# Which score pairs of an attention kernel go to VectorE: 66 instead of 62

## The chip, the cores and the metric

The kernel runs on one core of one Trainium2 chip. The metric is the device time of one execution in microseconds (us); smaller is better. The core has five engines with a queue of instructions each: PE (TensorE, matmuls into PSUM), ScalarE (ACT), VectorE (DVE), GpSimd (POOL) and SyncE (SP, which here issues most of the DMAs). Each queue is processed in order; semaphores tie the queues together.

## The reference, cut to what matters

Two branches read the same input x (2048 tokens, width 640) and are mixed by a gate:

```
g = sigmoid(sum(x * gate_w))
a = q * (long_conv(k_shift * v, ssm_k) + k_shift * v * D)      # A: state-space branch, q = x
p = softmax(scores * 20**-0.5)                                 # B: attention, 32 heads of 20,
b = (p @ v) @ wo                                               #    one shared k and v head
out = g * a + (1 - g) * b
```

In branch B every one of the 32 heads has 2048 x 2048 scores, and each of them needs one exponential: 134 million in all. The change is about which engine computes some of them.

## The kernel before, in words

**Tiles, groups, pairs.** A *group* G (0 to 31) is four heads by 512 query tokens: eight groups of heads for each of four blocks of queries. Inside a group, j (0 to 15) runs over blocks of 128 key tokens and r (0 to 3) over the heads. A score tile (G, j, r) is 128 keys by 512 queries, so there are 32 x 16 x 4 = 2048 tiles. Two tiles of one (G, j) are a *pair*; there are 1024.

**The main path.** Scores are multiplied by PE (L1023) into PSUM, two banks at a time for one unit and three for the next. ScalarE takes the exponential of a whole unit in one instruction (L1055): three tiles (1536 columns) into the buffer ETA, two tiles (1024 columns) into ETB, in turn. PE then multiplies by v (L1097) and sums over j in one PSUM bank, bank 6; a column of ones in v gives the denominator. With the last j of a group the sum is copied to `acc` (L1151), the denominators go through a short chain of DMAs (den, scr_d, rbc), their reciprocals are taken (L1156), and L1163 multiplies them in.

**VectorE's share.** For the pairs that the table `DVE_J` names, two of the four tiles of (G, j) never go to ScalarE. PE writes their scores into a side bank, and VectorE computes the exponential with six instructions: L1085 twice (out of PSUM into dJ), L1088, L1090, L1092 (the exponent's bits and a polynomial), L1093 (the product, into ETd, of which there is one buffer). PE adds ETd to the sum whenever it is there (L1097), at the latest before the last j of the group. `DVE_J[G]` lists the j of group G. All other tiles are strung together over the group borders and cut into units:

```
if j in DVE_J[G]:
    mine, rest = order[:2], order[2:]
    self.on_dve[G, j] = tuple(sorted(rest))
    order = rest + mine
...
n = 2 if len(self.units) % 2 else 3
self.units.append(tiles[i:i + n])
```

**The side work.** Branch A runs beside attention: a shift convolution on PE (L1270), the transforms of five chunks of channels (L1336) whose results VectorE evacuates (X and K, L1347 to L1355), complex products on GpSimd (L1367), inverse transforms on PE (L1400) with evacuation on VectorE (L1410). Projections of the next queries (L949), the output projection of the finished query blocks (L1434, evacuated by L1437 into outsb, then stored), and of six of the last block's groups (L1187, evacuated by L1191) are side work too. After the last accumulation a closing sequence runs alone: L1201 to L1206 on VectorE normalise the last group, PE multiplies (L1211), VectorE combines (L1233), and the last four stores go out.

**The order.** The order of each queue is not written by hand. A planner in the kernel builds a graph of all operations, gives each a cost from a small formula and a priority, and plays them through; the order in which it placed them is the order of each queue. In time that PE has left it puts filler matmuls (L1482). So another table `DVE_J` changes the place of nearly all the side work on PE, VectorE, GpSimd and SyncE, though not what is computed. The main sequence of scores and exponentials stays as the table and the units give it.

## Time and profile before

| what | value |
|---|---|
| time, median of 5 runs | 918.82 us (912.05 to 920.36) |
| the profiled execution's own time | 912.05 us |
| its span, first to last instruction | 910.2 us |
| granted TensorE clock, mean | 0.998 |
| first exponential of the scores starts | 25.3 us |
| exponentials on ScalarE (L1055) | 385 into ETA, 385 into ETB |
| pairs on VectorE (L1093) | 62 |

A row of the profile names the source line, the engine, the operation, what it writes and reads, and how often it ran; behind the bars stand its busy time, the mean duration of one, and the idle time of the engine just before it with what ended that. The chain of waits is followed back from the last instruction. The five runs contain the profiled one, which was the shortest; the other four lie between 918.31 and 920.36 us.

### The profile page before, as it was taken

The page shows a single profiled execution, that of the slowest core. Times are in us where ns is not written, and L with a number is a line of the kernel's source. Part 1 is how long each engine was busy: PE and PEld are TensorE (multiplying, and loading weights), DVE is VectorE, ACT ScalarE, POOL GpSimd, SP SyncE. Part 2 cuts the span into 40 slices and gives each one's busy share as a digit, 9 for nine tenths or more (in the row PEclk, how much of TensorE's full clock was granted, in tenths as well). Part 3 has the DMA queues.
Part 4 walks back from the last instruction along what each step waited for, and adds up shares of the span by engine and source line. Part 5 has one row for each costly group of instructions (what it writes and reads, how often), then busy time and mean ns, then how long its engine had stood idle before and what let it go on. Part 6 is the DMA issues. An engine that isn't in the chain of part 4 may idle for free.

```text
span 910.2 us, 16382 instructions
## 1 busy us (share of the span) xinstructions
PE 864.5 (95%) x7015; PEld 352.6 (39%) x7015; DVE 609.6 (67%) x854; ACT 887.8 (98%) x794; POOL 369.8 (41%) x330
## 2 busy tenths in 40 slices
PE   7999999999999999999999999999999989998997
PEld 3344434444343343443343334444444434422232
DVE  5467564459978766866576766566488655886673
ACT  5999999999999999999999999999999999999995
POOL 2940055790434477033576404569505871000000
PEclk9999999999999999999999999999999999999999
DMA  7930300010000001000001010000000003011100
GB/s 162 205 128 9 64 21 19 14 30 18 20 19 14 19 16 35 19 19 19 13 15 35 28 46 19 13 12 15 19 19 19 13 6 103 13 35 63 42 27 30
DMA packets 58507, 32.69 MB, mean 36 GB/s; under 512 B 41154, under 2 KB 54466, under 8 KB 58434
## 3 DMA queue, kind: packets, MB, share of 16 engines
q1 hardware_dynamic: 56168, 31.05, 12.4%
q8 instruction: 55, 0.90, 0.4%
q10 hardware_dynamic: 2266, 0.59, 0.3%
q14 instruction: 18, 0.15, 0.1%
HBM read 18.01 MB, written 6.02 MB: 26 GB/s over the span
## 4 chain that ended last, share of the span: by engine, by line
ACT 70%; PE 27%; DVE 1%; DMA 1%; SPq 1%; issue 0%; DVEq 0%
ACT ETA L1055 42%; ACT ETB L1055 28%; PE ps L1023 8%; PE ps L1336 6%; PE ps L1097 5%; PE ps L1400 3%; PE ps L949 2%; PE ps L1270 1%; DVE ETd L1093 1%; DMA xT<-in_A_q_dram 1%; SPq L722 1%; PE ps L893 0%; PE ps L965 0%; PE ps L1482 0%; PE ps L1211 0%; DVE outsb L1233 0%
## 5 line engine op out<-in xcount | busy, mean ns | idle before, releaser
L1055 ACT ACTIVATE ETA<-ps 128x1536 bf16<-128x1536 f32 x385 | 570.4, 1482 | 2.1 <-PE ps L1023 1.0
L1055 ACT ACTIVATE ETB<-ps 128x1024 bf16<-128x1024 f32 x385 | 408.7, 1062 | 0.1
L1023 PE MATMUL ps<-qT,kT 21*128 21x512 bf16 x2048 | 303.5, 384 | 30.8 <-ACT ETA L1055 20.8
L1367 POOL TENSOR_TENSOR Pp<-X,K 128x512 f32<-128x512 bf16 x120 | 162.9, 1383 | 350.6 <-DVE K L1355 349.6
L1097 PE MATMUL ps<-ETA,vaug 128*32 128x512 bf16 x1155 | 195.6, 389 | 0.3 <-ACT ETB L1055 0.3
L1097 PE MATMUL ps<-ETB,vaug 128*32 128x512 bf16 x769 | 186.8, 389 | 0.0
L1023 PEld LDWEIGHTS ps<-qT,kT 21*128 21x128 bf16 x2048 | 75.2, 91 | 226.1 <-ACT ETA L1055 120.9
L1085 DVE TENSOR_SCALAR dJ<-ps 128x512 uint32<-128x512 f32 x124 | 85.2, 687 | 38.7 <-PE ps L1023 38.1
L1093 DVE SCALAR_TENSOR_TENSOR ETd<-dJ,dE 128x1024 bf16<-128x1024 f32 x62 | 85.8, 1384 | 24.1 <-PE ps L1097 23.8
L1090 DVE SCALAR_TENSOR_TENSOR dE<-dJ,dE 128x1024 f32<-128x1024 uint16 x62 | 82.9, 1337 | 0.3
L1092 DVE SCALAR_TENSOR_TENSOR dJ<-dJ 128x1024 f32<-128x1024 uint16 x62 | 81.5, 1314 | 0.2
L1367 POOL TENSOR_TENSOR AB<-Pp 128x256 bf16<-128x256 f32 x80 | 79.1, 989 | 5.3
L1400 PE MATMUL ps<-AB,Tcos 128*128 128x256 bf16 x320 | 78.1, 275 | 0.0
L1097 PEld LDWEIGHTS ps<-ETA,vaug 128*32 128x32 bf16 x1155 | 47.8, 93 | 66.2 <-issue 63.9
L1400 PE MATMUL ps<-AB,Tsin 128*128 128x256 bf16 x280 | 69.2, 275 | 0.0
L1097 PEld LDWEIGHTS ps<-ETB,vaug 128*32 128x32 bf16 x769 | 45.0, 93 | 43.8 <-issue 42.2
L1367 POOL TENSOR_TENSOR Pp<-Pp 128x512 f32<-128x512 f32 x40 | 58.1, 1453 | 2.9
L1088 DVE TENSOR_SCALAR dE<-dJ 128x1024 uint32<-128x1024 uint32 x62 | 53.6, 865 | 0.6
L1151 DVE COPY acc<-ps 128x512 f32<-128x512 f32 x31 | 21.4, 689 | 48.2 <-PE ps L1097 48.1
L1336 PE MATMUL ps<-ssm_kT,Tsin 128*128 128x256 bf16 x320 | 53.0, 275 | 0.0
L1336 PE MATMUL ps<-ssm_kT,Tcos 128*128 128x256 bf16 x320 | 51.8, 275 | 0.0
L1336 PE MATMUL ps<-kv,Tcos 128*128 128x256 bf16 x320 | 51.7, 275 | 0.0
(135 smaller groups left out, 849.7 us busy)
## 6 DMA issues: line engine op xcount, KB each, us to landing
rbc<-scr_d SPq DMA_DIRECT2D x31, 256.0 KB
scr_o<-oTn SPq DMA_DIRECT2D x24, 128.0 KB, 1.7
xn<-in_A_q_dram SPq DMA_DIRECT2D x4, 640.0 KB
kv<-in_A_v_dram SPq DMA_DIRECT2D x4, 640.0 KB, 4.6
out_dram<-outsb SPq DMA_DIRECT2D x14, 160.0 KB, 2.3
oTp<-scr_o SPq DMA_DIRECT2D x12, 160.0 KB, 2.3
wog<-in_B_wo_dram SPq DMA_DIRECT2D x4, 200.0 KB
wo<-in_B_wo_dram SPq DMA_DIRECT2D x4, 200.0 KB
```

The lines of the kernel that those rows point to most:

```text
L1023: return e.matmul(self.bank(bk), T["kT4"][32 * r:32 * r + 21, 128 * j:128 * j + 128], T[f"qT{G // 8 % 2}"][32 * r:32 * r + 21, G % 8, :], ...
L1055: op("act", lambda e: e.activation(et(n)[:, 0:w], self.ps[:, lo:lo + w], ACT.Exp, scale=SCALE), [("ps", base[n % 2] + k) for k in range(le ...
L1085: self.evac(gr, "dve", lambda e, bk, h=h: e.tensor_scalar(J[:, 512 * h:512 * h + 512], self.bank(bk), SCALE * LOG2E * 65536.0, EOFF * 6553 ...
L1088: V(lambda e: e.tensor_scalar(E[:, :], J[:, :], 7, 0x7F800000, ALU.logical_shift_left, ALU.bitwise_and), [kJ], ["dE"], c_fast(1024), **k)
L1090: V(lambda e: e.scalar_tensor_tensor(Ef, lo, ED, Ef, ALU.add, ALU.mult), [kJ, "dE"], ["dE"], c_ps(1024), **k)
L1092: V(lambda e: e.scalar_tensor_tensor(Jf, lo, EP, lo, ALU.add, ALU.mult), [kJ], [kJ], c_ps(1024), **k)
L1093: V(lambda e: e.scalar_tensor_tensor(T["ETd"][:, :], Jf, EQ, Ef, ALU.add, ALU.mult), [kJ, "dE"], ["ETd"], c_ps(1024), **k)
L1097: return op("pe", lambda e: e.matmul(self.bank(6)[32 * r:32 * r + 32, :], T["vaug"][:, j, :], src, start=(j == 0), stop=(j == NSC - 1), ti ...
L1151: self.dve(lambda e: e.tensor_copy(T["acc"][:, :], self.bank(6)), [("ps", 6)], ["acc"], c_ps(512), prio=-9000.0, name="acc")
L1336: o = self.mm(gr, lambda e, bk, lhs=lhs, rhs=rhs, comp=comp, n=n: e.matmul(self.bank(bk, 256, 256 * comp), lhs, rhs, start=(n == 0), stop= ...
L1367: f = lambda e: e.tensor_tensor(out, a, b, alu)
L1400: self.mm(gr, lambda e, bk, lhs=lhs, fc=fc, comp=comp, h=h: e.matmul(self.bank(bk, 256, 256 * h), lhs, AB[:, fc, :, comp, :], start=(fc == ...
```

## The change

Only the table `DVE_J` differs. It names 66 pairs instead of 62, and most groups name other j than before. The first five groups now name none (before, groups 3 and 5 named one each); groups 11, 18 and 29 name four (before, group 6 alone did); the other groups name one to three. The table was found by a search on the planner.

```
-DVE_J = [(), (), (), (6,), (), (2,), (3, 7, 11, 13), (2, 6, 11), (2, 9), (2, 9), (2, 9), (2, 9), (3, 8, 13), (2, 9), (2, 9), (2, 9), (2, 9), (2, 9), (4, 11), (2, 9), (3, 9), (2, 9), (2,), (3, 8, 13), (2, 9), (2, 7), (2, 9), (2, 7, 12), (3, 8, 13), (3, 9), (3, 8, 13), (2, 7, 12)]
+DVE_J = [(), (), (), (), (), (6,), (2, 9), (2, 9), (2, 9), (2, 9), (2, 9), (3, 7, 11, 13), (2, 9), (6,), (3, 8, 13), (2, 9), (3, 9), (2, 9), (3, 7, 11, 13), (2, 7, 12), (2, 7), (3, 9), (2, 7), (1, 5, 9), (2, 7, 12), (3, 8, 13), (4, 11), (2, 6, 11), (2, 6, 11), (1, 4, 8, 12), (2, 9), (1, 5, 9)]
```

The changed program's order has 66 x 2 = 132 score tiles off ScalarE instead of 124. Nothing else of the source moves; everything that the planner decides is placed anew.

## The prediction

> **What bounds the kernel now.** I read the page first (busy shares, the chain that ended last), then the ScalarE timeline in one quiet stretch and at the start, then the waits, then VectorE by stage, and last the end of the program.

> ```profile
> PE 864.5 (95%) x7015; PEld 352.6 (39%) x7015; DVE 609.6 (67%) x854; ACT 887.8 (98%) x794; POOL 369.8 (41%) x330
> ...
> ACT 70%; PE 27%; DVE 1%; DMA 1%; SPq 1%; issue 0%; DVEq 0%
> ...
> L1055 ACT ACTIVATE ETA<-ps 128x1536 bf16<-128x1536 f32 x385 | 570.4, 1482 | 2.1 <-PE ps L1023 1.0
> L1055 ACT ACTIVATE ETB<-ps 128x1024 bf16<-128x1024 f32 x385 | 408.7, 1062 | 0.1
> ```

> ScalarE is busy 98% of the span, and its two exponentials stood idle 2.1 and 0.1 us in all before 770 instructions. Nothing that VectorE or PE does in between is felt as long as this stays so. The chain's 27% on PE does not contradict it: matmuls of one unit lie between two exponentials while the previous exponential still runs.

> ```profile
> 810.35 1.47 ACT L1055 ACTIVATE ETA<-ps 128x1536 bf16<-128x1536 f32 x1
> 811.67 1.05 ACT L1055 ACTIVATE ETB<-ps 128x1024 bf16<-128x1024 f32 x1
> 812.61 1.46 ACT L1055 ACTIVATE ETA<-ps 128x1536 bf16<-128x1536 f32 x1
> ```

> Here the instructions overlap: a three-tile unit is followed after about 1.33 us (not 1.47), a two-tile unit after 0.9 to 0.94 us (not 1.05). So what an exponential costs is its distance to the next, not its duration. The view of the tile ETA has first and last start at 25.3 and 898.9 us: 384 steps of three plus two tiles in 873.6 us, 2.275 us for five tiles, 0.455 us for one.

> ```profile
> PEld ps L1023 <- ACT ETA L1055: 120.9, 355, 1.2
> ...
> PEld ps L1023 <- ACT ETB L1055: 84.3, 290, 0.8
> ...
> DVE acc L1151 <- PE ps L1097: 48.1, 21, 6.9
> ...
> DVE ETd L1093 <- PE ps L1097: 23.8, 25, 1.8
> ...
> ACT ETA L1055 <- PE ps L1023: 1.0, 2, 0.8
> ```

> PE waits for ScalarE, 205 us at the weight loads of the scores; ScalarE waits for PE twice. Nearly all of the 24 us that VectorE sat before ETd was for PE to consume the previous ETd: VectorE runs ahead of need.

> **The change part by part.**

> *ScalarE.* 62 pairs are 124 tiles off ScalarE, 66 are 132. The 2048-124 = 1924 tiles on ScalarE are now 385 units of three, 384 of two, and one last unit of one tile in ETB. The changed 2048-132 = 1916 = 383 x 5 + 1 are 383 units of three, 383 of two, and one last unit of one tile, now in ETA. The order of the changed program agrees: ScalarE's list differs only in its last instructions. Removed: two three-tile units and one two-tile unit: 2 x 1.33 + 0.94 = 3.6 us (8 x 0.455 = 3.64 gives the same). The last one-tile unit costs the same in either tile. All of this is on the path: **-3.6 us**.

> *VectorE.* Four more pairs, each two L1085, one L1088, L1090, L1092 and L1093. Groups of VectorE's instructions in two stretches, 795 to 880 us, where GpSimd is idle, and 480 to 580 us, where it works:

> ```profile
> L1085 DVE TENSOR_SCALAR dJ<-ps 128x512 uint32<-128x512 f32 x16 | 11.0, 690 | 3.7 <-PE ps L1023 3.7
> L1093 DVE SCALAR_TENSOR_TENSOR ETd<-dJ,dE 128x1024 bf16<-128x1024 f32 x9 | 11.0, 1221 | 3.7 <-PE ps L1097 3.7
> ```
> ```profile
> L1093 DVE SCALAR_TENSOR_TENSOR ETd<-dJ,dE 128x1024 bf16<-128x1024 f32 x7 | 9.8, 1405 | 2.2 <-PE ps L1097 2.1
> ...
> L1088 DVE TENSOR_SCALAR dE<-dJ 128x1024 uint32<-128x1024 uint32 x7 | 5.5, 787 | 0.0
> ```

> Quiet, a pair is 2 x 0.690 + 0.676 + 2 x 1.216 + 1.221 = 5.7 us; beside GpSimd 2 x 0.687 + 0.787 + 1.418 + 1.263 + 1.405 = 6.2 us. Four pairs: 23 to 25 us on an engine that is idle 910.2-609.6 = 300 us. What hides it is local: in a group with n pairs ScalarE needs (64-2n) x 0.455 us, 25.5 for four, 26.4 for three, 27.3 for two. I counted VectorE's instructions in the changed order from one copy of acc (L1151) to the next and priced them so. The fullest groups are 29 (four pairs, six output evacuations, GpSimd done by then): 23.9 us of 25.5; 19: 23.3 to 25.5 of 26.4; 18 (four pairs): 22.2 to 24.3 of 25.5; 25: 21.9 to 23.7 of 26.4. These durations overlap by nearly 0.1 us each, 2 us a group. The kernel before already has such a group: group 6, four pairs, 25.0 us by the same prices in 25.5, and from 199.8 to 226.4 us ScalarE was busy 26.55 of 26.60. So I take **0** for VectorE. Cover gone, a group that overruns delays ETd, then PE's last accumulation and the next scores, by the overrun: 0 to 1 us in each of four groups. It cannot gain: ScalarE does not wait for VectorE now.

> *PE.* No matmul is added. Each pair splits a four-row accumulation into two of two (+4 slots) and issues its two scores alone (+8), and three units of scores go (-3): nine slots. PE's filler matmuls (L1482) follow each other at 0.22 us (three busy 0.82, one 0.385), so 2.0 us, against 149 fillers left in the changed order (151 now), 33 us that PE idles deliberately. **0**; at most 2.0 us if not one of them hit free time.

> *GpSimd.* [...] Row first: beside GpSimd L1093 is 1405 against 1221 ns and L1088 787 against 676, so 0.5 us a pair, slowing but no exclusion. [...] The page's waits give the cover: GpSimd waited 349.6 us for the spectra (POOL Pp, DVE K). [...] I use the row.

> *SyncE.* In the changed order the first loads of oTp and wo stand between the den transfer of group 26 and its scr_d, and two rounds of them before rbc; now all stand behind rbc. Rounds started 2.5 to 4.2 us apart (755.1, 757.8, 762.0, 764.5), so that group's rbc is up to 6 us later; queued behind it is L1163 and all after it on VectorE. Normally acc is free long before the next copy, 26 us later. VectorE may stop 0 to 3 us there. I take 0 on ScalarE, 1 us as the upper end.

> *The end.* Now side work is over at 891 us and the closing sequence starts alone:

> ```profile
> 890.35 0.55 DVE L1191 SCALAR_TENSOR_TENSOR part<-ps,omgf,kv 128x320 f32<-128x320 f32 x1 [1.17 <-PE ps L1187]
> 901.39 0.72 DVE L1201 STREAM_TRANSPOSE acc<-ps 128x512 f32<-128x512 f32 x1 [10.49 <-PE ps L1097]
> ...
> 904.47 3.26 DVE L1233 SCALAR_TENSOR_TENSOR outsb<-ps,omgf,part 128x640 bf16<-128x640 f32 x4 [0.60 <-PE ps L1211]
> ```

> In the changed order eight half blocks of the output projection (L1434, 40 matmuls) have moved into the last group. Five L1434 stand between the last two accumulations on PE, where three fillers (0.82 us) stand now, and their evacuation L1437 directly before L1201. Nearest row: L1437, 547 ns. The matmuls (5 x 0.135 us, by columns from the filler's 0.22) fit the fillers' place; then the evacuation overlaps the wait for the last accumulation (0.5 us from exponential's end to L1201). Bounds 0 and 0.6 us, no gain possible, since L1201 waits for that accumulation anyway; I take **+0.2**, as most is covered. The fourth L1233 must wait for the store of the same outsb: a store lands 2.3 us after issue, L1233's fourth starts 5.5 us after L1201: 0, up to 1 us if stores queue.

> *Sum.* -3.6 + 0.2 = -3.4 us. The profiled execution took 912.05 us (span 910.2 and 1.9 around it): 908.6. Its four unprofiled companions took 918.3 to 920.4, and the median is 918.82; I carry the 6.8 us between as constant: **915.4 us**, -0.37%.

> **The rivals.** (1) *More than the sum.* Against the steps 1.33 and 0.904 (start to start, most of the steps) ScalarE loses some 16 us over the span in small hitches. If the new spread also smooths these by 2 us, the gain is 5 to 6 us: 913. Against: the groups lose 0.2 to 0.9 us each with no relation to their pairs. (2) *Gain eaten.* The upper ends above (VectorE 2, PE 1, SyncE 1) take it back: 917 to 919. (3) *Slower: the side work becomes the end.* The last inverse transform stands later in the order (128 L1400: now 45 in group 26 and 83 in 27; changed, 81 in 27 and 47 in 28), so the output projection runs to the last accumulation instead of ending 10.5 us before L1201. All its halves go through one PSUM bank: five matmuls of 0.135 us, their latency, an evacuation of 0.55: about 1.5 us a half. [...] For: no filler is left behind them, and GpSimd feeds them. Against: GpSimd finished at 755.07 with the first dependent inverse at 760.3, PE's last group carries 76 side matmuls of 0.135 us, 10 us, less than group 2 carries now (12 us by the same price), and of PE's eleven waits for outsb now the longest was 0.9 us. (4) *The change does less than it says*: excluded by the order.

> **How the numbers follow.** What a measurement here can tell from no change is about 0.5%, 4.6 us. Main case 0.67 (912.5 to 917.5), more 0.10, eaten 0.11, slower 0.12. Faster by over 0.5% (below 914.2): the better rival and a fifth of the main case, 0.23. Slower (above 923.4): 0.11. Within: 0.66. Range 910.8 to 920: the main case, the eaten one and part of rival 1, about 0.83; outside are rival 3 and a gain beyond 8 us.

> **What would show it.** Right: 383 + 383 full units, idle before ETA and ETB still under 4 us, five tiles still at 2.275, first exponential still at 25.3, last exponential 3.6 us earlier, L1201 within 0.7 us of it. Wrong: ScalarE waits for PE in groups 18, 19, 25 or 29, with PE waiting for ETd (VectorE overrun); L1163 waiting for rbc near 775 us (SyncE); L1201 more than 1 us behind the last exponential, with L1437 before it (rival 3).

## The result, and the profile after

The changed kernel takes 908.33 us (median of 27 executions, 907.17 to 913.05); the kernel before, on the same chip and in the same rounds, 917.78 us (48 executions, 909.96 to 929.49). The ratio is 0.992, 95% interval 0.9901 to 0.9939: the change is faster, by more than the forecast of 915.4 us said, and outside its range of 910.8 to 920 on the fast side. The medians stand 1.0% apart and the ratio says 0.8%, because the executions of before fall into two clusters (15 of the 48 at 912.5 us or less, 33 at 916.1 or more) and their median lies in the longer one; the means are 916.3 and 909.1. The ratio leaves out executions over 1.5% above the fastest of their kernel, here the one of 929.49 us.

The profiled execution of the changed kernel took 908.11 us (span 906.0), its mean granted TensorE clock was 0.999. From its page, the busy shares, the chain that ended last, and ScalarE's two groups of exponentials:

```profile
PE 863.2 (95%) x7013; PEld 350.7 (39%) x7013; DVE 632.4 (70%) x878; ACT 883.8 (98%) x791; POOL 380.1 (42%) x330
...
ACT 64%; PE 31%; DMA 2%; DVE 1%; SPq 1%; issue 0%; DVEq 0%
...
L1055 ACT ACTIVATE ETA<-ps 128x1536 bf16<-128x1536 f32 x384 | 571.0, 1487 | 3.4 <-PE ps L1097 2.1
L1055 ACT ACTIVATE ETB<-ps 128x1024 bf16<-128x1024 f32 x383 | 410.0, 1071 | 0.2 <-PE ps L1023 0.2
```

384 and 383 exponentials: 383 units of three, 383 of two, and the last single tile, as forecast. VectorE has gained 22.8 us of work (632.4 against 609.6); ScalarE still sits idle for only 3.6 us before 767 exponentials. By this page the kernel is what the forecast said it would be: bound by ScalarE, a little shorter.

The pair of profiles explains 3.9 us: 912.05 against 908.11. From the first exponential's start to the last one's end the two traces measure 875.58 us before and 873.19 after, so -2.4. The first exponential starts at 23.5 us instead of 25.3, which is not the change: the start of before had one stretch of 3.4 us at half the TensorE clock (12.6 to 16.0 us), and two further profiles of the changed kernel have it too, with a first exponential at 25.6 and 25.3. The rest, +0.2, lies behind the last exponential and outside the span. But the medians fell by 9.45 us. More than half of the gain lies in executions that the two profiles don't show. That is what the experiments had to find.

### The profile page after: what moved, and what is told of

It is laid out like the page before. It is cut to its first block, busy times and chain, and to the rows that moved or that the text cites. A ratio compares the mean times of both kernels' runs of the same rounds, so it can differ in the third digit from the quotient of the medians.

```text
span 906.0 us, 16396 instructions
## 1 busy us (share of the span) xinstructions
PE 863.2 (95%) x7013; PEld 350.7 (39%) x7013; DVE 632.4 (70%) x878; ACT 883.8 (98%) x791; POOL 380.1 (42%) x330
## 4 chain that ended last, share of the span: by engine, by line
ACT 64%; PE 31%; DMA 2%; DVE 1%; SPq 1%; issue 0%; DVEq 0%
ACT ETA L1055 39%; ACT ETB L1055 25%; PE ps L1023 9%; PE ps L1336 7%; PE ps L1097 6%; PE ps L1400 3%; PE ps L949 2%; PE ps L1270 1%; DMA rbc<-scr_d 1%; DMA xT<-in_A_q_dram 1%; PE ps L1434 1%; SPq L722 1%; PE ps L1187 1%; PE ps L893 0%; PE ps L965 0%
## 5 line engine op out<-in xcount | busy, mean ns | idle before, releaser
L1055 ACT ACTIVATE ETA<-ps 128x1536 bf16<-128x1536 f32 x384 | 571.0, 1487 | 3.4 <-PE ps L1097 2.1
L1055 ACT ACTIVATE ETB<-ps 128x1024 bf16<-128x1024 f32 x383 | 410.0, 1071 | 0.2 <-PE ps L1023 0.2
L1023 PE MATMUL ps<-qT,kT 21*128 21x512 bf16 x2048 | 302.5, 384 | 29.0 <-ACT ETA L1055 21.0
L1367 POOL TENSOR_TENSOR Pp<-X,K 128x512 f32<-128x512 bf16 x120 | 168.6, 1429 | 358.1 <-DVE K L1355 350.7
L1097 PE MATMUL ps<-ETA,vaug 128*32 128x512 bf16 x1150 | 196.1, 389 | 0.4 <-DVE acc L1151 0.3
L1097 PE MATMUL ps<-ETB,vaug 128*32 128x512 bf16 x766 | 188.1, 389 | 0.0
L1023 PEld LDWEIGHTS ps<-qT,kT 21*128 21x128 bf16 x2048 | 74.7, 91 | 223.2 <-ACT ETA L1055 123.1
L1085 DVE TENSOR_SCALAR dJ<-ps 128x512 uint32<-128x512 f32 x132 | 90.7, 687 | 43.8 <-PE ps L1023 43.5
L1093 DVE SCALAR_TENSOR_TENSOR ETd<-dJ,dE 128x1024 bf16<-128x1024 f32 x66 | 89.3, 1354 | 19.6 <-PE ps L1097 19.4
L1090 DVE SCALAR_TENSOR_TENSOR dE<-dJ,dE 128x1024 f32<-128x1024 uint16 x66 | 89.9, 1362 | 0.5
L1092 DVE SCALAR_TENSOR_TENSOR dJ<-dJ 128x1024 f32<-128x1024 uint16 x66 | 89.3, 1353 | 0.4
L1400 PE MATMUL ps<-AB,Tcos 128*128 128x256 bf16 x320 | 78.2, 275 | 0.7 <-DVE dJ L1085 0.6
L1097 PEld LDWEIGHTS ps<-ETA,vaug 128*32 128x32 bf16 x1150 | 47.7, 93 | 65.6 <-issue 62.9
L1400 PE MATMUL ps<-AB,Tsin 128*128 128x256 bf16 x280 | 69.3, 275 | 0.0
L1097 PEld LDWEIGHTS ps<-ETB,vaug 128*32 128x32 bf16 x766 | 45.2, 92 | 43.5 <-issue 42.8
L1367 POOL TENSOR_TENSOR Pp<-Pp 128x512 f32<-128x512 f32 x40 | 60.9, 1524 | 2.7
L1088 DVE TENSOR_SCALAR dE<-dJ 128x1024 uint32<-128x1024 uint32 x66 | 54.1, 820 | 0.5
L1336 PE MATMUL ps<-ssm_kT,Tsin 128*128 128x256 bf16 x320 | 53.7, 275 | 0.0
L1336 PE MATMUL ps<-kv,Tsin 128*128 128x256 bf16 x320 | 53.7, 275 | 0.0
L1336 PE MATMUL ps<-kv,Tcos 128*128 128x256 bf16 x320 | 51.9, 275 | 0.4 <-DVE dJ L1085 0.3
L1336 PE MATMUL ps<-ssm_kT,Tcos 128*128 128x256 bf16 x320 | 51.8, 275 | 0.3 <-DVE dJ L1085 0.3
```

Of the source, the lines that this page charges most:

```text
L1023: return e.matmul(self.bank(bk), T["kT4"][32 * r:32 * r + 21, 128 * j:128 * j + 128], T[f"qT{G // 8 % 2}"][32 * r:32 * r + 21, G % 8, :], ...
L1055: op("act", lambda e: e.activation(et(n)[:, 0:w], self.ps[:, lo:lo + w], ACT.Exp, scale=SCALE), [("ps", base[n % 2] + k) for k in range(le ...
L1085: self.evac(gr, "dve", lambda e, bk, h=h: e.tensor_scalar(J[:, 512 * h:512 * h + 512], self.bank(bk), SCALE * LOG2E * 65536.0, EOFF * 6553 ...
L1088: V(lambda e: e.tensor_scalar(E[:, :], J[:, :], 7, 0x7F800000, ALU.logical_shift_left, ALU.bitwise_and), [kJ], ["dE"], c_fast(1024), **k)
L1090: V(lambda e: e.scalar_tensor_tensor(Ef, lo, ED, Ef, ALU.add, ALU.mult), [kJ, "dE"], ["dE"], c_ps(1024), **k)
L1092: V(lambda e: e.scalar_tensor_tensor(Jf, lo, EP, lo, ALU.add, ALU.mult), [kJ], [kJ], c_ps(1024), **k)
```

## The experiments

Each execution comes with its mean granted TensorE clock, profiled or not. Set against the times it is the clue. In the 50 executions of the kernel before that ran beside the first four experiments, 39 had a clock of 0.989 or less, and these are the long ones (in the set below from 915.7 us on); the nine at 0.998 or more had a median of 912.2. A mean clock of 0.988 over 915 us amounts to some 22 us at half clock (estimate, 0.012 x 915 x 2). Of the 28 recorded executions of the changed kernel (one more than its median counts) none was at 0.989 or less, 21 were at 0.998 or more, with a median of 908.15. The theory: in most executions of the kernel before, the clock is taken down to half somewhere, which costs about 7 us, and the new table has removed the place where that happens. The rival: the executions differ for another reason (another chip, a late DMA), and the changed order is better throughout.

The expectations give the emptiest 3.4 us of PE as a share (39% in the kernel before, 48% after). They count the time that the columns of the matmuls take, 0.22 us for 512 columns, which is the distance at which fillers follow each other. The views below count the whole bars of the matmuls, 0.385 us for such a filler, so the same stretch reads higher: 2.08 of 3.40 us.

### The two kernels again, and a look at a long execution

`e1_before_again` and `e4_after_again`, later `e10_before_look` and `e11_after_third`, are unchanged copies.

> The kernel before, unchanged, to see its single executions with their granted clock. Clock theory: PE's matmuls leave one stretch of 3.4 us near 741 us only about 39% filled (the lowest of the kernel before; the lowest of the kernel after is about 48%); in some executions the clock is taken back there. Then executions fall in two clusters, about 910 to 912 us at a clock of 0.998 or more and about 916 to 921 us at 0.995 or less, and time falls with clock. Rival (the longer executions have another cause, a late DMA say): two clusters, but the same clock in both.

Measured: 917.54 us (22 executions, 910.22 to 932.36), ratio to the kernel before 0.9992 (0.9967 to 1.0017). Fifteen of the 22 were at a clock of 0.989 or less (915.7 us and more), four at 0.998 or more (910.2 to 912.1), three between at 914.2 to 914.6. Time goes with the clock nearly step by step. The profiled execution was again one of the short ones.

> The kernel after, unchanged, beside the others on the same chip. Both theories: 907 to 910 us with a few executions at 912 to 913 us; the longer ones at the lower clock.

Measured: 908.96 us (6 executions, 908.20 to 909.81), all six at 0.998 or more; ratio 0.9894 (0.9855 to 0.9932).

> The kernel before, unchanged, one more profile. Clock theory: in about four of five executions the clock is halved from about 745 us on. If this profiled execution is one of them, its granted clock is 0.5 from about 745 us for some 10 to 17 us, the groups 25 and 26 lose about 7 us there, the span is 915 to 918 us, and nothing else differs from the first profile. If it is a clean one, span 909 to 911 us at 0.998 or more, and it says nothing on the place. A rival (the long executions lose their time spread over the span, and the clock is an accompaniment): a long execution without such a place.

Measured: 928.26 us, clock 0.976; this time the profile caught it. The rows of PEclk, page of this execution, 40 slices of 23 us: a 6, and later a 7 and a 6, where all other slices have 9.

```profile
PEclk9999999999999999999996999999999976999999
```

The trace's own records of the clock put it at 0.5 of full speed from 489.2 us for 17.07 us and from 752.1 us for 27.31 us. Busy time by stretch, the 3.4 us before each of the two and then the two themselves (columns: stretch, length, then busy time and count of PE, weight loads, VectorE, ScalarE and GpSimd, then clock, DMA share, GB/s):

```profile
748.70:752.10 3.40, 1.99 (x20) 0.60 (x18) 1.59 (x4) 3.40 (x4) 3.40 (x5) 1.00 0.02 2
752.10:779.40 27.30, 26.83 (x122) 6.67 (x121) 14.16 (x14) 19.29 (x17) 8.86 (x6) 0.50 0.32 89
485.80:489.20 3.40, 2.56 (x21) 0.70 (x20) 2.01 (x3) 3.40 (x4) 3.40 (x3) 1.00 0.00 0
489.20:506.30 17.10, 16.74 (x74) 4.34 (x71) 4.60 (x9) 10.80 (x10) 6.32 (x7) 0.50 0.01 1
```

Read the busy times of ScalarE and of PE: at full clock ScalarE is busy for all of its 3.40 us; at half clock PE is busy nearly throughout (16.74 of 17.1) and ScalarE only 10.80 of 17.1 and 19.29 of 27.3. While the clock is halved, TensorE is the bound. What ScalarE's steps from one exponential to the next take above their base (1.33 and 0.904 us, as in the prediction) adds up to 8.5 us in groups 16 and 17 together (1.2 in the clean profile) and to 9.6 us in group 26 (0.5): 7.3 us for the spell of 17 us, 9.1 for the one of 27. Such a spell shows in ScalarE's timeline as exponentials that wait for matmuls, which the page before showed for about 2 us in all:

```profile
754.15 1.45 ACT L1055 ACTIVATE ETA<-ps 128x1536 bf16<-128x1536 f32 x1 [0.30 <-PE ps L1023]
755.63 1.02 ACT L1055 ACTIVATE ETB<-ps 128x1024 bf16<-128x1024 f32 x1
758.07 1.45 ACT L1055 ACTIVATE ETA<-ps 128x1536 bf16<-128x1536 f32 x1 [1.41 <-PE ps L1097]
```

And what went before: 1.99 us of matmuls in 3.40. PE's timeline of the same execution:

```profile
749.39 0.39 PE L1023 MATMUL ps<-qT,kT 21*128 21x512 bf16 x2 [0.20 <-ACT ETB L1055]
750.73 0.39 PE L1023 MATMUL ps<-qT,kT 21*128 21x512 bf16 x3 [0.96 <-ACT ETA L1055]
```

This is the border between groups 25 and 26. The last accumulation of a group has gone out and bank 6 is being copied by L1151, so the planner allows no filler there. The side banks have no work either: in the clean profile the last transform (L1336) ends at 741.3 us, the next inverse one (L1400) starts at 758.2, and GpSimd, which makes the products between them, is still busy for all of the stretch. PE has a scores unit of 0.39 us, then a hole of nearly 1 us, the same as in the clean profile (0.95 us, up to 743.69). The expectation is met in place (about 745 us by the clean profile's time; the spell at 489 us shifts it by 7 us). The spell is longer than expected (27.3 us, not 10 to 17) and dearer (9.1 us, not 7), and that a second, earlier one would be in the same execution was not expected.

> The changed kernel, unchanged, to stand beside the one with rbc first: 908 to 909 us, all or nearly all executions at a granted clock of 0.997 or more; the hitch of about 0.7 us in group 27 is there again.

Measured: 909.97 us (6 executions, 908.13 to 912.55), ratio 0.9899 (0.9852 to 0.9946); four at 0.998 or more; the two lowest clocks, 0.995 and 0.994, go with the two longest times. The changed kernel's advantage repeats.

### One stretch filled, the table untouched

`e5_62_onegap` is the kernel before with its own table. Only in that one hole (730 to 740 us of the planner's own time, near 743 us of the trace) may fillers now go to a free side bank:

```
-        sch = Scheduler(self.g)
+        sch = GapFiller(self.g); ...
+class GapFiller(Scheduler):
+    def pick_pe(self, t):
...
+        if op is None and LO < t < HI and self.main_started and not self.can_fill ...
+            for x in SIDE:
+                if gap > 0.1 and self.busy_in(t, 2.4) < FILL and not (
+                        self.bank_claimed[x] or self.bank_busy[x] or self.bank_ready[x] > t):
+                    op = Op("pe", lambda e, x=x: self.filler_on(e, x), c_mm(512), "c", "fill", 0.0)
...
+LO, HI = 730.0, 740.0
```

> The table of before, untouched; the planner may put fillers into a free side bank at the one group end near 741 us, and puts four there. PE's order is the same up to that place. Clock theory, in its narrow form (that one stretch is what takes the clock back): the executions at a clock of 0.989 or less, now four in five, fall to one in five or fewer, median 910.5 to 913 us. Rival (other stretches do it as well, or group 22's change did it through its new order): more than half still at 0.989 or less, median 916 to 918 us.

Measured: 911.81 us (22 executions, 910.17 to 917.67) against 918.48 for the kernel before beside it; ratio 0.9956 (0.9933 to 0.9979). None of the 22 is at 0.989 or less (one is at 0.990, the 917.67), where 35 of the 47 of before were. PE's timeline at the hole:

```profile
745.39 0.39 PE L1023 MATMUL ps<-qT,kT 21*128 21x512 bf16 x2 [0.20 <-ACT ETB L1055]
745.71 1.04 PE L1481 MATMUL ps<-Tcos,zeros 128*128 128x512 bf16 x4
746.73 0.39 PE L1023 MATMUL ps<-qT,kT 21*128 21x512 bf16 x3
```

Four matmuls that compute nothing, 1.04 us of them, take 6.7 us off the median. With no pair moved, this kernel has seven tenths of the whole gain of 9.45 us. PE's order is the same up to the hole; behind it, side matmuls and fillers on PE, and from 781 us on some of VectorE's work, stand earlier or later, and three more fillers run, so the hole is not quite the only difference. But a spell of half clock begins right behind this hole (e10), and two kernels below that fill it in other ways lose the long executions too. The rival in its broad form falls: what made most of the long executions long is this one stretch of PE.

### Moving the weak place

Two tables with one entry changed ask the same question from both sides. The first keeps 62 pairs:

```
-DVE_J = [..., (2, 9), (2,), (3, 8, 13), ...]     # groups 21, 22, 23 of before
+DVE_J = [..., (2, 9), (6,), (3, 8, 13), ...]
```

> The table of before with one entry changed: group 22 names j = 6 instead of 2. Still 62 pairs, but the stretch near 741 us is filled (no 3.4 us of PE under about 49%). Clock theory: the cluster at 916 to 921 us goes, the median is 910 to 912 us, 0.7% below before, with no pair added. Rival (it is the number of pairs or the spread as a whole): median stays at 917 to 919 us like before.

Measured: 912.13 us (14 executions, 910.22 to 917.53), ratio 0.9934 (0.9908 to 0.9961), none at 0.989 or less (one at 0.990, which is the 917.53). One entry of the table, with the number of pairs unchanged, brings about 6 us. Its profile happens to be that one execution:

```profile
483.90:487.30 3.40, 2.41 (x19) 0.71 (x18) 2.29 (x3) 3.40 (x4) 3.40 (x3) 1.00 0.00 0
487.70:504.80 17.10, 16.74 (x74) 4.34 (x71) 4.64 (x9) 10.80 (x10) 6.31 (x7) 0.50 0.01 1
```

It is the weak place near 489 us again, which the kernel before has as well (e10): one of 14 executions here, with the same 17 us and a price of 7.3 us in groups 16 and 17.

The second keeps the 66 pairs of the changed kernel, and gives it an empty stretch near 715 us:

```
-DVE_J = [..., (2, 7), (1, 5, 9), (2, 7, 12), ...]     # groups 22, 23, 24 of after
+DVE_J = [..., (2, 7), (3, 8, 13), (2, 7, 12), ...]
```

> The table of after with one entry changed: group 23 names 3, 8, 13 instead of 1, 5, 9. Still 66 pairs, but the new order has a 3.4 us stretch of PE near 710 us that is only about 37% filled. Clock theory: a cluster of executions about 7 us longer appears, 913 to 917 us at a clock of 0.995 or less, in about half of the executions or more; the shortest stay at 907 to 908 us. Rival (number of pairs): median stays at 908 to 909 us like after.

Measured: 911.67 us (22 executions, 909.24 to 932.62), ratio 0.9935 (0.991 to 0.9959). Seven of the 22 are at 0.989 or less, none reaches 0.998. Direction as expected, share smaller: half or more had been expected to drop, and the shortest to stay at 907 to 908. The other 15 have a clock of 0.993 to 0.997, so they seem to lose some of it too, but for a shorter time; no profile shows one of them. The profiled execution, 917.81 us, has two spells, one of 10.2 us from 479.3 us and this one from 718.2 us:

```profile
714.80:718.20 3.40, 2.15 (x19) 0.60 (x19) 2.79 (x5) 3.40 (x5) 1.68 (x2) 1.00 0.02 2
718.20:735.30 17.10, 16.77 (x79) 4.90 (x78) 10.73 (x13) 11.89 (x11) 8.41 (x6) 0.50 0.05 17
```

2.15 us of matmuls in 3.40, then 17 us of half clock; ScalarE's steps lose 6.6 us in group 25 (0.4 in the changed kernel's profile). So it is the placing of work, not the number of pairs, that makes or mends such a place; 66 pairs can have it and 62 pairs need not.

### How much the fillers and the pairs are worth

The planner puts a filler where PE's planned share of the last 2.4 us is under FILL. Three kernels change only that number: `e6_66_fill65` (table of after) and `e7_62_fill65` (table of before) have `FILL = 0.65` instead of 0.55, `e8_66_nofill` (table of after) has `FILL = 0.0`, no fillers at all.

> The table of after, with the planner's threshold for fillers raised from 0.55 to 0.65 (about half again as many fillers, the emptiest 3.4 us of PE at 52%). Clock theory: clock 0.998 or more in all executions, the few at 912 to 913 us go, median 907.5 to 908.5 us. Rival (fillers get into the way of scores): median over 909.5 us at full clock.

Measured: 909.36 us (10 executions, 908.58 to 911.17), ratio 0.9909 (0.988 to 0.9938). More fillers bring the changed kernel nothing; the expected 907.5 to 908.5 is missed by 0.9 us, and two of the ten are at 0.997. The rival's figure, over 909.5 us, is missed by 0.1.

> The table of before with the same threshold of 0.65. Clock theory: median 910 to 912 us, executions at 0.989 or less rare, 0.7% under before with no pair added; the difference to the other kernel with 0.65 is what four pairs are worth at full clock: 3.6 us by the exponentials left out, some 2.3 us by the fastest executions of before and after. Rival (pairs and spread): median 917 to 919 us.

Measured: 911.84 us (22 executions, 910.42 to 914.55), ratio 0.9938 (0.9917 to 0.9958), none at 0.989 or less. With more fillers the kernel before also keeps its clock, and then the other table, four pairs and their new places together, is worth 911.84 - 909.36 = 2.5 us.

> The table of after with no fillers inside the stream (threshold 0). Clock theory: the clock is taken back many times, mean clock 0.95 or less and 925 to 1000 us, for by the profiles seen so far each 17 us at half clock costs about 7 us. Rival (fillers don't matter for the clock): 907 to 910 us at 0.997 or more.

Measured: 976.51 us (two executions, 971.47 and 981.55), ratio 1.0635 (1.053 to 1.0739), clock 0.899 and 0.884. The page's row of the clock and of PE's busy share:

```profile
PE   5999999999999999999899989989989998998997
...
PEclk9899999999979779999988985797989776796599
```

PE shows nearly the same busy digits as with fillers, because the same matmuls take longer: the 2048 of L1023 read 422 ns on average against 384 in the changed kernel, and a filler's bar reads 0.61 us at half clock (e10, 752.91 us) where it reads 0.39 at full clock (744.56 us of the clean profile). Only the clock row tells that 15 spells of 3.4 to 37.5 us lie in this span. The 149 fillers of the changed kernel, 33 us of PE time on nothing, are worth about 68 us.

### The transfer behind the loads

In group 27 the profile after has the largest new stall of the stream of exponentials. Three views of the changed kernel: the chain that ended last, followed within 770 to 791 us (start, length, what); VectorE's timeline; ScalarE's timeline.

```profile
772.07 0.64 SPq L565
...
772.75 7.33 DMA rbc<-scr_d
...
780.10 0.69 DVE oT L1163
```
```profile
780.10 0.69 DVE L1163 TENSOR_TENSOR oT<-acc,rbc 128x512 bf16<-128x512 f32 x1 [1.58 <-DMA rbc<-scr_d]
```
```profile
789.29 1.45 ACT L1055 ACTIVATE ETA<-ps 128x1536 bf16<-128x1536 f32 x1 [0.68 <-PE ps L1097]
```

The rbc transfer of group 26 is issued behind two rounds of loads of oTp and wo, and takes 7.3 us among them; L1163 waits 1.58 us; VectorE, with two j of ETd due and inverse transforms to evacuate, then works almost without a gap until 788.8 us; nine us after L1163 PE waits for it and ScalarE 0.68 us for PE. `e9_66_rbcfirst` is the changed kernel with the first loads held until that rbc is out. Only SyncE's queue differs:

```
-                     writes=[("oTp", I % 2)], nbytes=163840, prio=-800, name="ld_oT")
+                     writes=[("oTp", I % 2)], nbytes=163840, prio=-800, name="ld_oT", after=[self.rbcs[26]])
...
-                     name="ld_wo")
+                     name="ld_wo", after=[self.rbcs[26]])
```

> The changed kernel, with the first loads of oTp and wo issued on SyncE behind the rbc transfer of group 26; every other engine's order is the same. SyncE theory: rbc of group 26 lands about 2 us or more earlier, L1163 of that group does not wait for it, group 27's hitch of about 0.7 us before ETA goes, the stream of exponentials is 0.7 to 0.9 us shorter than the changed kernel's (872.8 to 873.2 there), and the time 0.5 to 1 us lower at the same granted clock: about 907.5. Rival (the hitch in group 27 comes from the order of the side work there, rbc is an accident beside it): the hitch stays, 908.2 to 909.

Measured: 908.94 us (6 executions, 907.47 to 913.04) beside 909.97 for the copy of the changed kernel; ratio to before 0.9893 (0.9849 to 0.9937). In the same place of its profile L1163 starts without a wait, and the exponential that was late (0.76 us in the copy's profile) is not:

```profile
784.21 0.68 DVE L1163 TENSOR_TENSOR oT<-acc,rbc 128x512 bf16<-128x512 f32 x1
```
```profile
792.02 1.46 ACT L1055 ACTIVATE ETA<-ps 128x1536 bf16<-128x1536 f32 x1
```

In this execution group 27 loses 0.7 us apart from the step of 1.27 us that a short spell of half clock costs (3.4 us from 772.4); in the copy's profile it loses 1.3: 0.6 us come back. In the medians that is not visible as a difference of its own (at a clock of 0.998 or more 908.85 of five executions against 909.56 of four, and the changed kernel's three sets already lie at 908.2, 909.0 and 909.6). So it is shown that the loads delayed rbc and that L1163 waited for it. That the late exponential comes from there follows from the chain, but is not shown apart: 16 us before, the short spell had held ScalarE back by 1.27 us, more than the 0.76, which by itself gives VectorE and PE time to catch up. This kernel is not shown to beat the changed one, and the expected 907.5 is missed.

The same profile bears on the rival of a late DMA. It is the longest of its six executions, 913.04 us at a clock of 0.993, and its first spell (6.8 us from 42.0 us) follows a late load of branch A:

```profile
39.36 1.29 DVE L1274 TENSOR_TENSOR kv<-ps,kv 128x512 bf16<-128x512 f32 x2 [3.61 <-DMA kv<-in_A_v_dram]
```
```profile
40.43 0.39 PE L1023 MATMUL ps<-qT,kT 21*128 21x512 bf16 x3 [1.67 <-DVE kv L1274]
```

VectorE waits 3.61 us for the load, PE 1.67 us for VectorE, and the clock is halved from 42.0 us on. The profile of e5 has the same wait (3.54 us) and a spell from 43.3 us; in the two profiles of before and after there is neither. So a late transfer can lengthen an execution, and here too it does so by way of an empty stretch of PE (1.74 us of matmuls in the 3.41 us before e9's spell).

## Why the prediction was wrong

**The step that failed** is the last of the sum: "Its four unprofiled companions took 918.3 to 920.4, and the median is 918.82; I carry the 6.8 us between as constant". These 6.8 us were not a constant beside the kernel. They were the price of half clock in about three of four executions (at a clock of 0.989 or less: 98 of the 131 executions of before and its copies in and beside the experiments), set off mostly by one stretch of PE in the kernel before. The view of busy time by stretch could have shown the stretch. The kernel before, in the clean first profile, cut first into the windows of 3.4 us that its spell at 12.59 us fixes, then across them:

```profile
739.60:743.00 3.40, 2.77 (x25) 0.97 (x22) 1.60 (x3) 3.40 (x4) 3.40 (x5) 1.00 0.00 0
743.00:746.40 3.40, 2.68 (x22) 0.80 (x22) 1.71 (x1) 3.40 (x4) 3.40 (x4) 1.00 0.02 2
...
741.10:744.50 3.40, 2.08 (x20) 0.51 (x18) 1.60 (x3) 3.40 (x5) 3.40 (x5) 1.00 0.02 2
```

The hole at 743 us was there in that execution too, but the border of two windows fell into it, and each half had 2.7 us of matmuls. Cut from 741.1 to 744.5 it is the emptiest 3.4 us in that trace after the start, 2.08 us of matmuls; no other comes under 2.4. The changed kernel's emptiest stretch, wherever it is cut, has 2.35 to 2.51 us in its three profiles, in the first one here:

```profile
817.00:820.40 3.40, 2.50 (x19) 0.74 (x18) 1.53 (x3) 3.40 (x4) 0.00 (x0) 1.00 0.00 0
```

The sum then nearly closes with the experiments' medians: filling that stretch takes 918.48 to 911.81 (-6.7), and the table at a kept clock is 2.5 us (fillers at 0.65 in both), together -9.2 of the -9.45 measured. In the ratios the parts are 0.4% and 0.3% and the whole change is 0.8%: less than in the medians, because the median of before lies in the longer of its two clusters.

**ScalarE, -3.6.** The number and kind of the units removed are right, and so is the price per step (five tiles in 2.278 us after, 2.275 before). The stream shortened by 2.4 us in the profiled pair and by 2.8 in the second (e1 against e4). Small stalls above the base step grew from 15.8 to 16.9 us; these 1.1 us are nearly all that is missing.

**VectorE, 0: right.** The overrun of groups 18, 19, 25 and 29 didn't come: these groups lose 0.4 to 0.5 us each, as much as before. VectorE's waits at ETd for PE are still 19.4 us of its time.

**PE, 0 (to 2).** No sign of the nine slots; not tested by itself.

**SyncE, 0 with 1 us as upper end.** The mechanism was named rightly (rbc late, L1163 waiting; 1.6 us measured within the 0 to 3), the term mis-sized: about 0.6 us seem to have reached ScalarE, where 0 was taken.

**GpSimd, nothing in the sum: right.** From 480 to 580 us the changed kernel's pairs read 800 ns for L1088 and 1264 to 1428 ns for L1090 to L1093, against 681 and 1213 to 1216 ns from 795 to 880 us, where GpSimd is idle: slowed as in the row of before (787 and 1263 to 1418 ns), not shut out. GpSimd sat 7.2 us waiting for L1383 once and finished 12 us later than before (its last product starts at 765.0 instead of 753.4), and still the chain of the page after has no part on GpSimd.

**The end, +0.2: right.** L1437 runs just ahead of L1201 as the order said, and the columns of the timeline show how little it costs:

```profile
896.03 0.66 ACT L1055 ACTIVATE ETA<-ps 128x512 bf16<-128x512 f32 x1
...
896.88 0.55 DVE L1437 SCALAR_TENSOR_TENSOR outsb<-ps,omgf,kv 128x320 bf16<-128x320 f32 x1 [1.28 <-PE ps L1434]
897.35 0.71 DVE L1201 STREAM_TRANSPOSE acc<-ps 128x512 f32<-128x512 f32 x1
```

L1201 starts 0.66 us after the last exponential's end (896.03 + 0.66), 0.15 more than before.

**The rivals.** "More than the sum" named the right side with a wrong cause: it let the spread smooth ScalarE's small stalls, and these grew. "Gain eaten" happened in part, 1.1 us of 3.6. "The side work becomes the end" did not happen, and no run shows the 923.4 us from which it was counted: the longest execution of the changed kernel took 913.05. None of them looked at the clock, though the 6.8 us between the profiled time and the median were twice the forecast gain of 3.4.

**Not settled.** How empty a window must be. Counting matmul time (whole bars) in windows of 3.413 us (the length of the spell in the first profile), laid so that they end where a drop begins, and only after 25 us: in the kernels with fillers those up to 2.21 us were followed by half clock (1.74, 2.01, 2.13, 2.19, 2.21), with one exception at 2.14; one of 2.24 us in e1's profile was not; of those between 2.4 and 2.6 a few were (2.56, 2.58 twice) and most not; and two had 2.8 and 3.16. By the columns' time (0.22 us for 512 columns, from each matmul's start) all 13 profiles together split better: all 13 windows under 46% were followed by half clock (8 of them in the kernel without fillers), of those from 46 to 50% 5 of 22, up to 60% 6 of 287, and above that 1 of 2917. The hole of before has 39 to 40% in its two clean profiles (the first and e1's), the emptiest stretch of the changed kernel 44 to 49% in its three. So the columns' time comes close to what counts, but is not all of it: ahead of 25 us windows of 36 and 42% kept the clock (e2, e7), and some traces lack up to 1% of the matmul records, which makes some of their windows look emptier than they were. Nor was it tried why some spells last 3.4 us and others 17.

## What to carry to other kernels

When the profiled execution is shorter than its unprofiled companions, explain the difference before adding to it: compare the mean granted clock of all executions, and look for the emptiest 3.4 us of PE in the trace, wherever it is cut. This kernel is bound by ScalarE and still needs PE busy, for at half clock PE was the bound, for 17 us at a time (busy 16.74 of 17.1 us in e10, ScalarE 10.80). A change that only moves work, or four matmuls at a group's border that compute nothing, can be worth more than the work that another change saves.
